# State tokens of a maxout kernel: half of the slots of all eight batches in one tile, instead of all slots of four batches

## The chip, the cores and the metric

The kernel runs on one core of one Trainium2 chip. Its time is the device time of one execution in microseconds (us); several executions are timed and their median is given. One further execution was taken with the hardware profiler; all rows below come from that one. Engines are named as the profile names them: PE multiplies matrices, PEld loads its weights, DVE and ACT do element work and copies, POOL does copies and issues the casting loads, SP only issues DMAs and waits.

## The reference, cut to what matters

`x` has 8 batches, 8 heads, 512 tokens and 64 features a head; `state` has 32 slots in place of the 512 tokens. Each batch makes two attention reads, which stand one behind the other along the token axis, so that a batch has 512 + 32 = 544 rows of 512 features. Each row then goes through a maxout layer.

```python
scores  = scale * np.matmul(x, state.transpose(0, 1, 3, 2))
a       = softmax(scores)
xread   = np.matmul(a, state)                   # 8 x 8 x 512 x 64
scores2 = scale * np.matmul(state, x.transpose(0, 1, 3, 2))
a2      = softmax(scores2)
sread   = np.matmul(a2, x)                      # 8 x 8 x 32 x 64
attn_out = np.concatenate([xread, sread], axis=2)
x = attn_out.transpose(0, 2, 1, 3).reshape(8 * 544, 512)
h = np.maximum(np.maximum(x @ w1, x @ w2), x @ w3)   # 768 wide
return h @ w_out                                     # 4352 x 512, float32
```

The last 32 of each batch's 544 rows are the state tokens: 8 x 32 = 256 rows in all, 512 KB of the output.

## The kernel before

The work is a list of operations written out by hand (FIRST, EACH for batches 2 to 6, LAST), performed in that order; each engine's queue keeps the order, and the waits between engines follow from the tiles. Batches go through scores, exponentials, weights, transposes, the first layer (three matmul groups a piece of 128 features, `pw`, and a maximum over them by ACT and DVE into `ht`), the second layer (`po`) and a store of the rows (`osb`).

The state read of a batch (`sread`, `sread_scale`) gives 128 partitions (4 pairs of heads by 32 slots) by 128 features. A DMA transpose on SP (`sread_turn`, L343) turns it into `ats[:, b]`, with the features of a pair of heads on the partitions and 4 x 32 columns. `sread_place` (L348) then copies these 128 columns into `atp`, the state tokens of all batches: POOL does it for seven batches and ACT for batch 5. Of `atp` each of the 4 pairs of heads has 256 columns, one for a state token. In the kernel before, a column's place is (half j of the batches, slot n, batch within the half).

When all eight batches have been placed, the first layer for the state tokens runs in LAST (`l1s 0` to `l1s 5`, `layer1_states`): 6 pieces of 12 matmuls that stream all 256 columns of a pair of heads. The result `hts` is 128 x 6 x 256. The second layer takes 128 of the 256 columns at a time as weights (`l2p s j c0 c1`: tile j, features c0 to c1), so that row p of the result is column 128j + p of `atp`. The result is copied to `osb["s"][:, j, c0:c1]` by ACT or DVE (`layer2_part_out`, L463) and stored by `store_part` (L467): five DMAs, two on ACT's queue and three on SP's, of 128, 128, 256, 128 and 384 features. The last operation of LAST is the store of 384 features of tile 0 on SP, 128 rows of 1536 bytes.

`state_rows(j)` is the output side of these stores. Before, it is the 32 slots of four batches, slot outermost: 32 steps of 2048 bytes, in each 4 steps of a batch (544 x 2048 bytes). The other side is 128 partitions of `osb`.

Behind LAST stands a branch on `flag` to a fallback that is not taken in these runs (L593). It holds uses of the same functions with DVE copies (`sread_turn_mm`) and whole-row stores of the state tokens. After it, at L658, SP waits in turn for the completion of each DMA semaphore, and the engines meet at barriers; there the program ends.

Of the kernel before, what the change touches and what calls it, by code (L numbers as in the profile page):

```python
# [10 lines left out]
BF16 = mybir.dt.bfloat16  # L11
# [63 lines left out]
def kernel(  # L75
# [10 lines left out]
    nc = tc.nc  # L86

    B, H, S, D = x.shape
    _, _, Ns, _ = state.shape
    HD = H * D  # L90
    SP = S + Ns
# [5 lines left out]
    J = 4  # L97
    HS = H // 2
# [5 lines left out]
    data = ctx.enter_context(tc.tile_pool(name="data", bufs=1))  # L104
# [5 lines left out]
    copier = {"D": nc.vector.tensor_copy, "A": nc.scalar.copy, "P": nc.gpsimd.tensor_copy}  # L110
    times = {"D": nc.vector.tensor_mul, "P": nc.gpsimd.tensor_mul}
# [14 lines left out]
    ones = const.tile([128, 128], BF16, name="ones")  # L126
    warm = const.tile([128, 1], F32, name="warm")
    ats = data.tile([128, B, HS, Ns], BF16, name="ats")
    atp = data.tile([128, HS, 2, Ns, 4], BF16, name="atp")
    seen = data.tile([128, B, J * H + 2], F32, name="seen")  # L130
    flag = data.tile([128, 1], I32, name="flag")

    xT, e, a, aT, G, ht, osb, xp = {}, {}, {}, {}, {}, {}, {}, {}
    open_ps = {}

    def new(d, b, shape, name, bufs=2):
        d[b] = work.tile(shape, BF16, tag=name, bufs=bufs, name=name)
# [4 lines left out]
    def bank(shape, dtype, name):  # L142
        return pp.tile(shape, dtype, tag="b" + next(homes["b"]), bufs=1, name=name)
# [104 lines left out]
    def parity(v, g):  # L248
        return v if g is None else v[:, :, g:g + 1]
# [18 lines left out]
    rdens = {}  # L268
# [8 lines left out]
    def weights(b, g, c):  # L277
        if not g:
            new(a, b, [128, J, 2, HS, Ns], "a")
        n = 2 if g is None else 1  # L280
        times[c](  # L281
            out=parity(a[b], g).rearrange("p j g s n -> p j (g s) n"),
            in0=parity(e[b], g).rearrange("p j g s n -> p j (g s) n"),
            in1=rdens.pop((b, g)).rearrange("p j g s -> p j (g s)").unsqueeze(3).to_broadcast(
                (128, J, n * HS, Ns)))

    def a_turn(b, g):
        if g == 0:
# [56 lines left out]


    def sread_place(b, c):
        copier[c](out=atp[:, :, b // 4, :, b % 4], in_=ats[:, b])  # L348

    def sread_turn_mm(b):  # L350
        p = bank([128, HS, Ns], BF16, "prt")
        nc.tensor.transpose(p.rearrange("p s n -> p (s n)"), srs.pop(b).rearrange("p g d -> p (g d)"), ident)
        nc.vector.tensor_copy(out=atp[:, :, b // 4, :, b % 4], in_=p)

# [108 lines left out]
    def store_part(b, j, c0, c1, q):  # L465
        if b == "s":
            queue[q].dma_start(out=state_rows(j)[:, :, c0:c1], in_=osb[b][:, j, c0:c1])  # L467
            return
        queue[q].dma_start(
            out=out[b * SP:b * SP + S, :].rearrange("(p j) f -> p j f", j=J)[:, j, c0:c1],  # L470
            in_=osb[b][:, j, c0:c1])
# [4 lines left out]
            in_=osb[b][:, j0:j1, :])  # L476

    def state_rows(j):
        return out.rearrange("(b t) f -> b t f", t=SP)[4 * j:4 * j + 4, S:SP, :].rearrange("b n f -> n b f")

    def store_states(j, q):
        queue[q].dma_start(out=state_rows(j), in_=osb["s"][:, j, :])
# [16 lines left out]
    def set_flag():  # L499
# [13 lines left out]
        "warm": (warm_exp, 0), "busy": (keep_busy, 0), "stc": (states_cast, 0), "stt": (states_turn, 0),  # L513
        "stp": (states_place, 0), "xt": (x_turn, 1), "xtc": (x_turned, 1), "xtd": (x_turn_dma, 1),
        "sc": (scores, 1), "ex": (exps, 1), "sum": (sums, 1), "wt": (weights, 1), "at": (a_turn, 1),
        "atc": (a_turned, 1), "atd": (a_turn_dma, 1), "pad": (pad, 1), "sr": (sread, 1),
        "srs": (sread_scale, 1), "srt": (sread_turn, 1), "ap": (sread_place, 1), "g": (g_slice, 1), "gc": (g_sliced, 1),
        "gr": (g_run, 1), "grc": (g_ran, 1), "l1": (layer1, 1), "l1s": (layer1_states, 0),
        "m0": (max_first, 1), "ma": (max_second, 1), "mb": (max_third, 1), "l2": (layer2, 1), "l2c": (layer2_out, 1),
# [73 lines left out]
    with tc.If(bad != 0, label="again"):  # L593
        for b in range(B):
            for d in (xT, e, a, aT, G, ht, osb, xp):
                d.pop(b, None)
            for g, c in ((0, "A"), (1, "D")):
                x_turn(b, g)
                x_turned(b, g, c)
            scores_below_max(b)  # L600
            sums(b)
            weights(b, None, "D")
            for g, c in ((0, "A"), (1, "D")):
                a_turn(b, g)
                a_turned(b, g, c)
            if b >= 2:
                pad(b)
            sread_below_max(b)
            sread_scale(b)
            sread_turn_mm(b)  # L610
            for m in range(NM):
                g_slice(b, m)
                g_sliced(b, m, "A")
            for m in range(NM):
                layer1(b, m)
                max_first(b, m)
                max_second(b, m)
                max_third(b, m)
            for j in range(J):
                layer2(b, j)  # L620
                layer2_out(b, j, "A")
                store(b, j, j + 1, "P")
# [40 lines left out]
```

## Time and profile before

| what | value |
|---|---|
| median of 3 timed executions | 156.05 us (155.54 to 156.09) |
| the profiled execution, its own time | 155.43 us |
| its span, first to last instruction | 153.5 us |
| PE busy | 145.8 us (95% of the span) |
| DVE busy | 110.0 us (72%) |
| ACT busy | 85.4 us (56%) |
| POOL busy | 52.3 us (34%) |
| granted TensorE clock, mean | 0.991 |
| L348, placing the state read of a batch | POOL x7, 469 ns; ACT x1, 493 ns |
| L467, stores of state tokens | 5 DMAs, 544 to 666 ns to issue |

The time of an execution holds some 1.9 us that lie outside the span. An engine's busy time is the sum of its instructions; a wait is put down to whatever ended it. A DMA is issued by an engine's queue (SPq, ACTq, POOLq) and lands later, when all its parts have been written; the time to landing counts from the issue.

### The profile page before, as it was taken

To read this page: it belongs to the slowest core of one execution; us is meant where nothing else is said; L and a number is where in the kernel's file an instruction comes from. 1 tells how busy PE (TensorE), PEld (TensorE's weight loads), DVE (VectorE), ACT (ScalarE), POOL (GpSimd) and SP (SyncE) were. 2 spreads that over 40 slices of the span, in tenths; PEclk is the share of its full clock that TensorE was granted. 3 is DMA by queue.
4 is the path that set the end of the run, shared out by engine and by line. 5 is a ranking of instruction groups with operands and counts; after the bars stand their busy time and mean duration, and the time that the engine had idled before them with its cause. 6 is when DMAs were issued, how large, how long until landed. Compare 5 with 4: busy or idle time off the path is not lost.

```text
span 153.5 us, 3632 instructions
## 1 busy us (share of the span) xinstructions
PE 145.8 (95%) x1434; PEld 73.2 (48%) x1434; DVE 110.0 (72%) x192; ACT 85.4 (56%) x140; POOL 52.3 (34%) x72
## 2 busy tenths in 40 slices
PE   6998899999999999999999999999999999999970
PEld 2565344343444444444444444444444445679850
DVE  1678968899898887688768876887688666852530
ACT  3536687764747474747474747475747344434220
POOL 6979829103996100916037003700320100000000
PEclk9999999999999999999999999999999999999996
DMA  4999999899999999932956094507030700107351
GB/s 104 241 197 200 199 194 182 125 214 189 157 136 263 199 193 284 243 82 63 295 123 73 2 297 120 75 7 274 4 68 14 279 6 4 68 2 269 111 192 60
DMA packets 39269, 22.30 MB, mean 145 GB/s; under 512 B 22096, under 2 KB 37200, under 8 KB 39248
## 3 DMA queue, kind: packets, MB, share of 16 engines
q0 software_dynamic: 13584, 7.60, 35.9%
q1 hardware_dynamic: 23792, 10.56, 30.9%
q10 hardware_dynamic: 1872, 3.87, 6.6%
q8 instruction: 12, 0.20, 0.5%
q14 instruction: 9, 0.07, 0.2%
HBM read 15.20 MB, written 8.91 MB: 157 GB/s over the span
## 4 chain that ended last, share of the span: by engine, by line
PE 75%; DMA 16%; DVE 2%; POOL 2%; issue 1%; ACT 1%; POOLq 0%
PE pw L413 37%; PE po L444 24%; DMA x<-in_x_dram 9%; DMA wout<-in_moe_w_out_dram 7%; PE po L459 5%; PE pg L360 4%; PE ps L259 2%; PE psr L324 1%; POOL xp L308 1%; DVE seen L273 1%; PE pgh L360 1%; DVE xT L241 1%; POOL a L281 1%; PE idle L208 1%; PE pxt L234 0%
## 5 line engine op out<-in xcount | busy, mean ns | idle before, releaser
L413 PE MATMUL pw<-aT,G 128*128 128x512 bf16 x288 | 66.4, 379 | 0.0
L433 DVE TENSOR_TENSOR t<-t,pw 128x512 bf16<-128x512 bf16 (+1 forms) x54 | 35.3, 654 | 15.4 <-ACT t L428 12.8
L428 ACT CAST t<-pw 128x512 bf16<-128x512 f32 (+1 forms) x54 | 30.4, 562 | 27.6 <-PE pw L413 26.9
L413 PEld LDWEIGHTS <-G 128*128 128x128 bf16 x288 | 27.2, 98 | 33.2 <-issue 1.7
L444 PE MATMUL po<-wout,ht 128*128 128x512 bf16 x168 | 40.2, 380 | 0.1
L437 DVE TENSOR_TENSOR ht<-t,pw 128x512 bf16<-128x512 bf16 x48 | 32.8, 686 | 4.7
L281 POOL TENSOR_TENSOR a<-e,rden 128x1024 bf16<-128x1024 bf16 (+1 forms) x10 | 15.7, 1568 | 42.1 <-ACT G L400 30.0
L444 PEld LDWEIGHTS <-ht 128*128 128x128 bf16 x168 | 15.2, 98 | 20.0 <-issue 2.1
L400 ACT CAST G<-pg 128x1024 bf16<-128x1024 f32 x22 | 21.8, 1018 | 4.7 <-PE pg L360 4.7
L273 DVE TENSOR_REDUCE seen<-e 128x32 f32<-128x1024 bf16 (+1 forms) x10 | 10.0, 1003 | 5.3 <-ACT e L266 5.3
L308 POOL COPY xp<-x 128x1024 bf16<-128x1024 bf16 x12 | 12.5, 1076 | 3.6 <-DMA x<-in_x_dram 3.6
L451 DVE COPY osb<-po 128x512 f32<-128x512 f32 x17 | 11.4, 669 | 2.9 <-PE po L444 2.8
L266 ACT ACTIVATE e<-ps 128x1024 bf16<-128x1024 f32 (+1 forms) x10 | 8.4, 852 | 7.8 <-PE ps L259 7.8
L360 PE MATMUL pg<-w,bd 64*32 64x512 bf16 (+1 forms) x288 | 11.2, 363 | 0.9 <-DMA w<-in_moe_w_dram 0.9
L348 POOL COPY atp<-ats 128x128 bf16<-128x128 bf16 x7 | 3.2, 470 | 23.9 <-DMA ats<-sr 23.9
L451 ACT COPY osb<-po 128x512 f32<-128x512 f32 x11 | 6.5, 587 | 7.9 <-PE po L444 7.9
L167 POOL DMA_DIRECT2D x<-in_x_dram x13 | 10.1, 791 | 0.9 <-POOLq L647 0.9
L378 ACT CAST G<-pg 128x768 bf16<-128x768 f32 x10 | 8.0, 803 | 2.0 <-PE pg L360 1.9
L208 PE MATMUL idle<-zero 128*128 128x512 bf16 x25 | 7.6, 444 | 1.4 <-DVE zero L186 1.3
L413 PE MATMUL pw<-atp,w 128*128 128x256 bf16 x72 | 8.7, 273 | 0.0
L413 PEld LDWEIGHTS <-w 128*128 128x128 bf16 x72 | 6.9, 98 | 1.2
L463 ACT COPY osb<-po 128x128 f32<-128x128 f32 (+2 forms) x11 | 3.4, 315 | 6.8 <-PE po L459 6.7
(61 smaller groups left out, 100.8 us busy)
## 6 DMA issues: line engine op xcount, KB each, us to landing
x<-in_x_dram POOLq DMA_DIRECT2D x13, 256.0 KB, 9.4
out_dram<-osb ACTq DMA_DIRECT2D x6, 512.0 KB, 4.0
out_dram<-osb SPq DMA_DIRECT2D x5, 512.0 KB, 2.9
w<-in_moe_w_dram POOLq DMA_DIRECT2D x5, 256.0 KB, 9.3
w<-in_moe_w_dram POOLq DMA_DIRECT2D x2, 384.0 KB, 9.5
wout<-in_moe_w_out_dram POOLq DMA_DIRECT2D x1, 768.0 KB, 10.4
out_dram<-osb SPq DMA_DIRECT2D x3, 256.0 KB, 2.1
osb<-in_x_dram SPq DMA_DIRECT2D x1, 512.0 KB, 3.8
```

The source lines that it names most:

```text
L167: nc.gpsimd.dma_start(out=x_part(b, g), in_=x_heads(b, g))
L273: nc.vector.reduce_sum(out=den, in_=parity(e[b], g), axis=AX.X)
L281: times[c](out=parity(a[b], g).rearrange("p j g s n -> p j (g s) n"), in0=parity(e[b], g).rearrange("p j g s n -> p j (g s) n"), in1=rdens ...
L308: nc.gpsimd.tensor_copy(out=xp[b][:, :, :, g * (D + 1):g * (D + 1) + D], in_=v[:, g])
L360: nc.tensor.matmul(p(s, g), bd(b, 2 * s + g)[64 * g:64 * g + 64, g, :], f(w_sb[64 * g:64 * g + 64, s]), start=True, stop=True, tile_positi ...
L400: copier[c[g]](out=v[:, g:h], in_=p[:, g:h, 0:c1 - c0])
L413: nc.tensor.matmul(pw[i][:, 0:n], lhs(i, k), rhs(k), start=(k == 0), stop=(k == nk - 1))
L428: nc.scalar.copy(out=t0s[b, m][:, 0:n], in_=open_ps["l", b, m][0][:, 0:n])
L433: nc.vector.tensor_max(t1s[b, m][:, 0:n], t0s.pop((b, m))[:, 0:n], open_ps["l", b, m][1][:, 0:n])
L437: nc.vector.tensor_max(ht[b][:, m, :], t1s.pop((b, m))[:, 0:n], open_ps.pop(("l", b, m))[2][:, 0:n])
L444: nc.tensor.matmul(p, ht[b][:, m, j * 128:(j + 1) * 128], wout_sb[:, m, :], start=(m == 0), stop=(m == NM - 1))
L451: copier[c[i]](out=o[:, j, i * w:i * w + w], in_=p[:, i * w:i * w + w])
```

## The change

`atp` has its 256 columns in another order: (half j of the slots, batch, slot within the half), so a tile of 128 state tokens is 16 slots of all eight batches, batch outermost. The copies at L348 (and the DVE copies of the fallback) write runs of 16 neighbouring columns instead of single columns at a distance of 4. The output side of the state stores becomes 8 batches (steps of 544 x 2048 bytes) outermost and in each 16 neighbouring rows (steps of 2048 bytes). The number of matmuls, copies and stores, their order on every queue and their waits are the same. `weights` gets a form that can deal its work to several engines; every call in the lists names one engine, for which the loop runs once and issues what was issued before.

```diff
-    atp = data.tile([128, HS, 2, Ns, 4], BF16, name="atp")
+    atp = data.tile([128, HS, 2, B, Ns // 2], BF16, name="atp")
...
     def weights(b, g, c):
         if not g:
             new(a, b, [128, J, 2, HS, Ns], "a")
-        n = 2 if g is None else 1
-        times[c](
-            out=parity(a[b], g).rearrange("p j g s n -> p j (g s) n"),
-            in0=parity(e[b], g).rearrange("p j g s n -> p j (g s) n"),
-            in1=rdens.pop((b, g)).rearrange("p j g s -> p j (g s)").unsqueeze(3).to_broadcast(
-                (128, J, n * HS, Ns)))
+        n, r = 2 if g is None else 1, rdens.pop((b, g))
+        for i in range(len(c)):
+            j = slice(i * J // len(c), (i + 1) * J // len(c))
+            times[c[i]](
+                out=parity(a[b], g)[:, j].rearrange("p j g s n -> p j (g s) n"),
+                in0=parity(e[b], g)[:, j].rearrange("p j g s n -> p j (g s) n"),
+                in1=r[:, j].rearrange("p j g s -> p j (g s)").unsqueeze(3).to_broadcast(
+                    (128, J // len(c), n * HS, Ns)))
...
     def sread_place(b, c):
-        copier[c](out=atp[:, :, b // 4, :, b % 4], in_=ats[:, b])
+        copier[c](out=atp[:, :, :, b], in_=ats[:, b].rearrange("p s (j n) -> p s j n", j=2))
 
     def sread_turn_mm(b):
...
-        nc.vector.tensor_copy(out=atp[:, :, b // 4, :, b % 4], in_=p)
+        nc.vector.tensor_copy(out=atp[:, :, :, b], in_=p.rearrange("p s (j n) -> p s j n", j=2))
...
     def state_rows(j):
-        return out.rearrange("(b t) f -> b t f", t=SP)[4 * j:4 * j + 4, S:SP, :].rearrange("b n f -> n b f")
+        return out.rearrange("(b t) f -> b t f", t=SP)[:, S + Ns // 2 * j:S + Ns // 2 * (j + 1), :]
```

## The prediction

> **What bounds the kernel now.** I read the page's busy times and its chain first, then the groups that touch `atp` and the state stores (L348, L467), then SP's waits and the last five microseconds in order of time.
>
> ```profile
> span 153.5 us, 3632 instructions
> PE 145.8 (95%) x1434; PEld 73.2 (48%) x1434; DVE 110.0 (72%) x192; ACT 85.4 (56%) x140; POOL 52.3 (34%) x72
> ...
> PE 75%; DMA 16%; DVE 2%; POOL 2%; issue 1%; ACT 1%; POOLq 0%
> ```
>
> PE is the bound from its first matmul to its last. The change gives PE not one instruction more or less, so it can act in two places only: where PE waits for `atp`, and behind PE's last matmul. First the copies into `atp` and their readers (duration in ns: shortest, median, longest; then first and last start):
>
> ```profile
> L348 POOL COPY atp<-ats x7: 469/469/471, 61.5 to 122.7; 128x128 bf16<-128x128 bf16 x7
> L348 ACT COPY atp<-ats x1: 493/493/493, 126.5 to 126.5; 128x128 bf16<-128x128 bf16 x1
> ...
> L413 PE MATMUL pw<-atp,w x72: 272/273/273, 128.8 to 143.4; 128*128 128x256 bf16 x72
> ```
>
> POOL's last copy ends at 123.2 us, ACT's at 126.95, and PE first reads `atp` at 128.75: 5.6 and 1.8 us to spare. Next the end. These are the last instructions in order of time (start, duration), and SP's wait for the last store:
>
> ```profile
> 147.79 0.81 PE L459 MATMUL po<-wout,hts 128*128 128x384 bf16 x4
> 147.96 0.26 PEld L459 LDWEIGHTS <-hts 128*128 128x128 bf16 x2
> 148.12 0.39 SPq L469 DMA_DIRECT2D out_dram<-osb  x1
> 148.65 0.48 ACT L463 COPY osb<-po 128x384 f32<-128x384 f32 x1 [2.21 <-PE po L459]
> 149.15 0.54 SPq L467 DMA_DIRECT2D out_dram<-osb  x1
> ```
>
> ```profile
> SPq L658 <- DMA out_dram<-osb: 0.5, 1, 0.5
> ```
>
> ```profile
> L467 SPq DMA_DIRECT2D out_dram<-osb x3: 544/658/666, 146.5 to 149.1; - x3
> ...
> L467 ACTq DMA_DIRECT2D out_dram<-osb x2: 547/592/637, 146.3 to 147.6; - x2
> ...
> DMA to landing us min/median/max: 2.1/2.2/3.4
> ```
>
> PE ends at 148.6, ACT copies the last 128x384 piece, SP issues its store at 149.15, and 4.4 us more pass to the end. In them two things run side by side. SP loads the flag, takes the branch and checks one DMA semaphore after another; it reaches that of the last store at 152.04. The store itself lands 3.4 us after its issue, at 152.53, though the median state store lands after 2.2. So the end hangs on this store, but only by the 0.5 us in SP's wait; behind it lie another 0.98 us of barriers.
>
> The packets in the trace tell why it is late. It is 128 packets of 1536 bytes. On each of the 16 DMA engines eight run one behind the other, 61 ns apart, as in the 128x384 store before it whose output has 128 rows in one step. Of the store's 16 completions twelve come from 151.21 to 151.35 us; then stragglers at 151.71, 151.91, 152.06 and 152.53. The last one's engine fetched a 16 KB block of instructions from 149.25 to 150.79 (a packet of the instruction queue of 1541 ns), then did the eight rows of the store ahead (landing 151.97), and only then these eight. The one at 152.06 was held up in the same way behind an 8 KB fetch.
>
> **The change, part by part.**
>
> *Copies into `atp`.* Eight copies change form: the same 128 columns, now 8 runs of 16 in place of single columns 4 apart. No row shows the new form. Below: the 128x1024 POOL copy (L308) takes 1076 ns, so (1076 - 469) / 896 = 0.68 ns a column and 383 ns fixed; a copy falls to 383 at the least, -0.09 us. Above: the whole 1076 ns of that row, +0.61 us. I take 469, the row with the same number of columns. Either end is covered on POOL: behind its copies stand only later batches' copies and weights, and it idles 23.9 us ahead of three of the copies for their DMA. On ACT one copy is behind cover of 0.71 us, its idle time ahead of the next copy of `po` at 127.66, and of 1.8 us to PE. Cost: nothing. If ACT's took over 1.2 us, that copy would start late, and beyond 2.3 us PE would.
>
> *Matmuls and layers.* 72 matmuls at 272 ns read the same 256 neighbouring columns; which token a column is changes no shape. The `hts` maxima (410 to 422 ns), the second layer and the copies L463 are as they were. `weights` issues the same ten instructions. Waits on all queues are unchanged. Cost: nothing, with no cover needed.
>
> *Issue of the five state stores.* Now 544 to 666 ns on the queue. The nearest rows are those of L469, whose output has 128 steps in one dimension: 332 to 426 ns. The new output has two dimensions like the old one. Bounds: -0.21 us (544 - 332) and +0.12 (666 - 544) for each; I take 0, the row with two dimensions. ACT's stores have nothing urgent behind them. SP has 0.64 us idle between the issue of the store at 148.12 and that at 149.15, so only the last store's own issue is on the path.
>
> *Transfer of the last store.* Rows, bytes and packet size are as before; how they are dealt to the DMA engines may not be. The output's outermost count was 32, dealt to 16 engines at two each; it becomes 8. Bounds: still 16 engines at 8 rows, +0; or one engine for each outermost step, eight at 16 rows, 8 x 61 = +0.49 us on each engine used. No row of this trace has an outermost count under 16, so neither is shown. I take eight engines, because the old 32 is dealt out evenly and 8 can't be dealt to 16 without splitting a step. The skill speaks against this change here: the Trainium skill, DMA: Bandwidth & Descriptors, section "Why a DMA increments its semaphore by 16 and not by 1", has the number of engines as the largest up to 16 that divides the slowest dimensions of both sides. By that rule 32 and 128 gave 16 engines, with which the trace's 16 chains of eight packets agree, and 8 and 128 give eight; the sum by the rule has the +0.49, without it +0.
>
> What 0.49 us costs depends on which engines these are. An undisturbed engine lands at 151.35 + 0.49 = 151.84, before SP looks at 152.04: hidden. If the engine that ended last (152.53) is used, it lands at 153.02: +0.49 at the end. If it is not used but the one of 152.06 is, that lands at 152.55: +0.02. If neither is, SP finds everything landed at 152.04: -0.49, and that is a floor, since the store ahead, still on all 16 engines, lands at 151.97. Engines start a store in a fixed order, seven within 27 ns and nine 53 to 145 ns after the first; in a store on ACT at 142.89 the engine behind on account of the previous fetch is missing among the nine. The one held up by the 8 KB fetch is missing among the seven. If the eight that are used are about the seven that start first, the late one drops out and the 8 KB one stays: +0.02. I take this, for want of a better sign.
>
> *The four earlier state stores.* They last landed at 149.72 and the queue is empty between them: 16 rows of 512 bytes at 24 ns are 0.19 us more, 16 of 1024 bytes 0.34 more, all before SP asks.
>
> Sum: 0 + 0 + 0 + 0.02 on the profiled execution's 155.43 us (span 153.5 and 1.93 outside). The median of the runs, 156.05, is 0.62 above that execution; the same difference on the median gives 156.1.
>
> **The rivals.** A difference of 0.5%, 0.78 us, is about what a measurement of this kernel can tell from no change.
>
> A. *The late engine is among the eight.* For: half of 16 engines are used, and the code fetch will come again at the same place. Against: the order of starts above. +0.49: 156.54, still within 0.5%.
>
> B. *Slower for good: a row takes longer.* An engine's 16 rows now come from 16 neighbouring partitions and go to one 32 KB stretch of the output, instead of to four batches; if that halves its speed, 122 ns a row, the store takes 16 x 122 = 1.95 us for 0.49. An undisturbed engine would land at 152.81, +0.28; the late one, if used, at 153.99, +1.46: 157.5. For: in the disturbed stretch of the tail single packets do take 107 to 399 ns. Against: rows of 1536 bytes take 61 ns both in the store to four batches and in the 128-row store. It passes 0.5% with the late engine used and 16r - 0.49 > 0.78, at r = 79 ns a row.
>
> C. *Faster: both held-up engines drop out.* -0.49, and -0.21 more if the issue falls to 332 ns, because SP's own chain then starts that much earlier: -0.70, 155.35. Against: the two stand in different groups of starts, so eight of 16 rarely miss both.
>
> D. *The store still goes to 16 engines.* +0: 156.05. For: every store in the trace does.
>
> **How the numbers follow.** Chances: the forecast 0.40, A 0.24, B 0.15, C 0.12, D 0.09. In C half lies beyond 0.5% with the spread of the runs (155.54 to 156.09): faster 0.06. B, and the tenth of A that this spread carries over (0.03), make slower 0.18. The rest is 0.76. The range goes from C without the cheaper issue, 155.55, to A with half of the runs' spread (0.27) on top, 156.8; left out are most of B and the end of C, about 2 in 10.
>
> **What would show it.** Copies at L348 between 383 and 1076 ns with PE's first read of `atp` no later after the matmul before it. State stores whose packets run in eight chains of 16, not 16 of eight, 61 ns apart for 1536 bytes. Issue of L467 near 0.55 to 0.66 us. SP's wait for the last store: about 0.5 us as forecast, 1.0 in A, none in C. The forecast is wrong if PE's last matmul moves, or if SP's checks before the last one move: the branch's own code fetch would then compete with longer stores.

## The result, and the profile after

The changed kernel takes 156.97 us (median of 22 executions) beside 156.04 us for the kernel before (22 executions, taken in turns). The ratio is 1.0052, 95% interval 1.003 to 1.0075: slower, by about half of one per cent. The ratio and its interval leave out three of the 22 executions of the changed kernel, which fell into a slower state that both kernels show now and then; without them its median is 156.58 us. A second series gave 1.0045 (1.0008 to 1.0082). The prediction was 156.1 us, with 155.55 to 156.8 as its range.

From the page of the changed kernel: its span, its busy times and the DMA queues of SP (q1) and ACT (q10), with packets, MB and share of 16 engines' time:

```profile
span 154.4 us, 3632 instructions
PE 146.0 (95%) x1434; PEld 73.3 (48%) x1434; DVE 109.9 (71%) x192; ACT 85.1 (55%) x140; POOL 51.5 (33%) x72
...
q1 hardware_dynamic: 23768, 10.56, 30.4%
q10 hardware_dynamic: 1856, 3.87, 6.6%
```

The same two lines of the kernel before:

```profile
q1 hardware_dynamic: 23792, 10.56, 30.9%
q10 hardware_dynamic: 1872, 3.87, 6.6%
```

All engines work as long as they did; the span is 0.9 us longer. The bytes are equal, but q1 has 24 packets less and q10 has 16 less. SP issues three state stores and ACT two, and in the traces every DMA engine that takes part in a store ends its share with one small packet of 4 bytes. Each store has lost eight of these (3 x 8 on q1, 2 x 8 on q10): it runs on 8 engines and not on 16.

The copies into `atp` and their reader in the changed kernel:

```profile
L350 POOL COPY atp<-ats x7: 287/291/293, 61.4 to 122.7; 128x128 bf16<-128x128 bf16 x7
L350 ACT COPY atp<-ats x1: 311/311/311, 126.5 to 126.5; 128x128 bf16<-128x128 bf16 x1
...
L415 PE MATMUL pw<-atp,w x72: 272/273/273, 128.8 to 143.4; 128*128 128x256 bf16 x72
```

The copies are 0.18 us shorter and PE reads no sooner: 128.8 us in both kernels. Next the end in order of time, then SP's waits at L660 (L658 before; sum, times, longest), then the issue of the state stores (ns: shortest, median, longest):

```profile
148.17 0.34 SPq L471 DMA_DIRECT2D out_dram<-osb  x1
148.69 0.48 ACT L465 COPY osb<-po 128x384 f32<-128x384 f32 x1 [2.21 <-PE po L461]
149.19 0.61 SPq L469 DMA_DIRECT2D out_dram<-osb  x1
```

```profile
SPq L660 <- DMA out_dram<-osb: 1.1, 2, 0.9
```

```profile
L469 SPq DMA_DIRECT2D out_dram<-osb x3: 609/612/762, 146.5 to 149.2; - x3
...
L469 ACTq DMA_DIRECT2D out_dram<-osb x2: 614/900/1187, 146.3 to 147.6; - x2
```

Up to the issue of the last store the kernels are alike to 0.05 us (149.15 and 149.19). Everything that was lost lies behind it: SP waits 0.9 us for the last store where it was 0.5, and it comes to that wait later. From the trace's packets and completions of the last store:

| us from the last store's issue | before | changed | changed, second profile |
|---|---|---|---|
| engines | 16 | 8 | 8 |
| first row starts | 1.21 | 1.25 | 1.25 |
| rows over 80 ns, longest | 4, 349 ns | 28, 568 ns | 27, 521 ns |
| first completion | 2.06 | 3.11 | 3.07 |
| store ahead (16 engines) completes | 2.82 | 3.30 | 2.86 |
| last completion | 3.38 | 4.23 | 4.07 |
| SP's flag load takes | 0.998 | 1.252 | 1.295 |

A row is one packet of 1536 bytes, and a completion is an engine's report that its share has landed. The earliest of the engines is already 1.0 us later than before, and the last one 0.7 to 0.85.

### The profile page after: what moved, and what is told of

The parts are those of the page before. It is cut to its first block, busy times and chain, and to the rows that moved or that the text cites. A ratio compares the mean times of both kernels' runs of the same rounds, so it can differ in the third digit from the quotient of the medians.

```text
span 154.4 us, 3632 instructions
## 1 busy us (share of the span) xinstructions
PE 146.0 (95%) x1434; PEld 73.3 (48%) x1434; DVE 109.9 (71%) x192; ACT 85.1 (55%) x140; POOL 51.5 (33%) x72
## 4 chain that ended last, share of the span: by engine, by line
PE 79%; DMA 12%; DVE 2%; POOL 2%; ACT 1%; issue 0%; DVEq 0%
PE pw L415 37%; PE po L446 24%; DMA wout<-in_moe_w_out_dram 7%; DMA x<-in_x_dram 6%; PE po L461 5%; PE pg L362 4%; PE idle L208 4%; PE ps L259 2%; PE psr L326 1%; POOL xp L310 1%; DVE seen L273 1%; PE pgh L362 1%; DVE xT L241 1%; POOL a L283 1%; PE pxt L234 1%; PE pt L219 1%
## 5 line engine op out<-in xcount | busy, mean ns | idle before, releaser
L350 POOL COPY atp<-ats 128x128 bf16<-128x128 bf16 x7 | 2.0, 290 | 24.1 <-DMA ats<-sr 24.0
```

## The experiments

The runs are to tell these theories apart. **N**: the number of engines, and with it the rows on each, sets the end. **P**: rows are slow because of where eight batches' rows go. **F**: slow rows come from what the branch sets off. Four more came up on the way, all on why an engine's first rows are slow: **A** and **O** (the distance between the engines' addresses in the output), **E** (eight engines as such) and **R** (the partitions that are read). Theory A is not the prediction's rival A.

### The changed kernel again

No edit.

> The changed kernel once more, for a second look at its tail. Theory N (number of engines: the five state stores run on 8 DMA engines with 16 rows each, and the end follows the latest of these): 8 completions for each state store, SP's wait for the last store near 0.9 us as in the first profile, time +0.8 us (+0.5%) over before. Theory P (place: rows are slow because eight batches' rows, 544 x 2048 bytes apart, are written at the same time): the same time, but rows of the state stores at over 61 ns (1536 bytes) throughout the store, also where no instruction fetch or flag load is under way.

1.0045 (1.0008 to 1.0082), 156.67 us. SP's wait:

```profile
SPq L660 <- DMA out_dram<-osb: 0.9, 1, 0.9
```

As N expects, in the time, in the wait and in the 8 engines of each state store. The slow rows come at the start only; from the fifth row of an engine on they take 61 ns, so the form of P with slow rows throughout falls.

### Half of the slots, slot outermost

```diff
-    atp = data.tile([128, HS, 2, B, Ns // 2], BF16, name="atp")
+    atp = data.tile([128, HS, 2, Ns // 2, B], BF16, name="atp")
...
-        copier[c](out=atp[:, :, :, b], in_=ats[:, b].rearrange("p s (j n) -> p s j n", j=2))
+        copier[c](out=atp[:, :, :, :, b], in_=ats[:, b].rearrange("p s (j n) -> p s j n", j=2))
...
-        return out.rearrange("(b t) f -> b t f", t=SP)[:, S + Ns // 2 * j:S + Ns // 2 * (j + 1), :]
+        return out.rearrange("(b t) f -> b t f", t=SP)[:, S + Ns // 2 * j:S + Ns // 2 * (j + 1), :].rearrange("b n f -> n b f")
```

> Tiles of half of the slots of all eight batches as in the change, but slot outermost and batch within, so the output side is 16 steps of 8. Theory N: 16 completions for each state store, 8 rows on an engine, the last store lands about 3.3 us after its issue or earlier, time as before within 0.3% (ratio 0.997 to 1.003). Theory P: eight batches are still written side by side, the time stays at the change's +0.5%. The copies into atp go back to about 470 ns (columns 8 apart) in both.

0.9963 (0.9929 to 0.9997): the price is gone. Tiles hold the same tokens as in the change; only the order within a tile went back to slot outermost. The copies, the landing of the state stores and SP's wait:

```profile
L350 POOL COPY atp<-ats x7: 755/757/919, 61.9 to 123.1; 128x128 bf16<-128x128 bf16 x7
L350 ACT COPY atp<-ats x1: 777/777/777, 127.0 to 127.0; 128x128 bf16<-128x128 bf16 x1
```

```profile
DMA to landing us min/median/max: 2.1/2.3/3.6
```

```profile
SPq L660 <- DMA out_dram<-osb: 0.5, 1, 0.5
```

There are 16 completions a store and SP's wait is 0.5 us again. P falls as well: the eight batches are still written side by side, and the price is gone. The copies are not "about 470 ns" as expected but 757 (columns 8 apart, where the kernel before had them 4 apart), and it costs nothing that the time shows. The first rows of the last store took up to 199 ns here, on 16 engines: a slow start isn't a matter of eight engines alone.

### All slots of four batches, batch outermost

```diff
-    atp = data.tile([128, HS, 2, Ns, 4], BF16, name="atp")
+    atp = data.tile([128, HS, 2, 4, Ns], BF16, name="atp")
...
-        copier[c](out=atp[:, :, b // 4, :, b % 4], in_=ats[:, b])
+        copier[c](out=atp[:, :, b // 4, b % 4], in_=ats[:, b])
...
-        return out.rearrange("(b t) f -> b t f", t=SP)[4 * j:4 * j + 4, S:SP, :].rearrange("b n f -> n b f")
+        return out.rearrange("(b t) f -> b t f", t=SP)[4 * j:4 * j + 4, S:SP, :]
```

> Tiles of all slots of four batches as before the change, but batch outermost, so the output side is 4 steps of 32. Theory N: 4 completions for each state store, 32 rows on an engine, 32 x 61 = 1.96 us a store where it was 0.49: an undisturbed engine ends the last store at about 152.8 us of the span, a late one at 154.0 or more; time +1.0 to +2.3 us over before (ratio 1.006 to 1.015), more than the change. Theory P: four batches as before, time as before (ratio 0.998 to 1.002).

1.0194 (1.0128 to 1.026), 159.1 us: 3.1 us over before, more than N's upper end. Its profiled execution took 167.68 us, where the others took 158.66 to 160.62, and in it PE waits 5.1 us for a DMA near 50 us; so only its tail is read:

```profile
SPq L658 <- DMA out_dram<-osb: 3.5, 3, 2.5
```

```profile
q1 hardware_dynamic: 23756, 10.56, 27.8%
q10 hardware_dynamic: 1848, 3.87, 6.4%
```

These are another 12 and 8 packets less than in the change: four engines a store. The last store lands 6.7 us after its issue; its 32 rows on an engine start three microseconds after the issue, behind the stores ahead of it, and the first take up to 342 ns. The direction and the order (16, 8, 4 engines: 0, +0.5, +1.9%) are N's; the size shows that rows on an engine at 61 ns are not the whole price, since N's upper end of 2.3 us was reckoned with them.

### Both kernels without flag load, branch and fallback

```diff
-    bad = nc.values_load(flag[0:1, 0:1], min_val=0, max_val=1,
-                         skip_runtime_bounds_check_because="flag is the result of a comparison")
-    homes["b"], homes["w"] = cycle("0123"), cycle("01")
-    with tc.If(bad != 0, label="again"):
...
-                store_states(j, "P")
```

> The changed kernel without the flag's loads, the branch and the fallback behind it (the fallback is left out, the rest is whole). No engine loads the flag and none jumps. Theory N: the 16 rows of each engine in the last store run at 61 ns from the first to the last, it lands about 2.7 us after its issue (2.2 of the median state store before plus 0.49), and the end hangs on it. Theory F (fetches: the rows that took 107 to 568 ns in the change's last store were slowed by what the branch sets off): no row over 80 ns here. Theory P: rows over 80 ns here too.

> The kernel before without the flag's loads, the branch and the fallback (left out, the rest is whole). Theory N with F: 16 engines, 8 rows at 61 ns, no stragglers beyond 0.2 us; the run is shorter than the changed kernel without the fallback by 0.4 to 0.6 us, that is by the eight rows more (0.49) and not by the 0.9 us that the two kernels' profiles differ by. Theory P: shorter by 0.8 us or more.

Changed: 155.62 us, 0.9949 (0.9894 to 1.0003) of the kernel before; before: 154.41 us, 0.9857 (0.9812 to 0.9903). SP's waits at the end, of the changed kernel, then of the kernel before, both without the fallback:

```profile
SPq L571 <- DMA out_dram<-osb: 2.1, 2, 1.8
```

```profile
SPq L569 <- DMA out_dram<-osb: 0.8, 1, 0.8
```

Here the change costs 1.2 us (four executions of each), more than in the whole kernel and more than the 0.4 to 0.6 of N. Without the branch the kernel before has no straggler: 16 completions from 2.04 to 2.30 us after the issue, no row over 65 ns. The changed kernel's last store completes from 3.05 to 3.65 us after the issue, and 29 of its rows take over 80 ns, up to 418. F falls: with no branch and no code fetch within the store's rows the slow rows are there. What P had named for these two runs, slow rows and 0.8 us or more, did come, but its reason had fallen with the slot outermost. The fallback hides a part of the price. With it the last store of the kernel before lands 3.38 us after its issue and not 2.30, because one of its 16 engines fetches code first; the changed store lands after 4.23 and 4.07 and not 3.65, a smaller loss, and its eight engines don't include the one of the longest fetch (see below).

### The state store not last

```diff
-    sop s 0 384 512 A; l2p 7 2 256 512;
-    l2pc 7 2 256 512 D; l2p s 0 0 384; sop s 1 128 256 S; sop s 1 256 512 S; sop 7 2 256 512 S;
-    l2pc s 0 0 384 A; sop s 0 0 384 S;
+    sop s 0 384 512 A; l2p s 0 0 384;
+    l2pc s 0 0 384 A; l2p 7 2 256 512; sop s 1 128 256 S; sop s 1 256 512 S; sop s 0 0 384 S;
+    l2pc 7 2 256 512 D; sop 7 2 256 512 S;
```

> The changed kernel with the last two pieces exchanged: the 384 features of state tile 0 are multiplied, copied and stored ahead of the 256 features of batch 7's tile 2, so a store of 128 rows in one dimension (16 engines, 332 ns to issue, 46 ns a row) comes last. Theory N: the state store's 16 rows run beside the last piece's matmuls, and the change's price falls by more than half: ratio to before 0.997 to 1.002. If instead the end hangs on SP's own chain of loads and checks, it ends as the change does.

> The kernel before with the same exchange. Theory N: 16 engines either way; the issue of the last store falls from 544 to 332 ns, its rows from 61 to 42 ns, and the piece ahead of it is 128x256 instead of 128x384 to copy (0.42 on DVE against 0.48 on ACT): up to 0.5 us less than before, ratio 0.996 to 1.0. If stragglers alone set the end, as before within 0.2%.

> The kernel before with the last two pieces exchanged, again, to narrow its interval: the store of state rows no longer comes last. The first look gave 0.9964 (0.9929 to 1.0). If the gain is that of the shorter last store, 0.996 to 0.999; if it was the spread of the stragglers, 0.999 to 1.001.

On the changed kernel: 1.0002 (0.996 to 1.0044) of the kernel before, within N's expectation; the interval is too wide to say how much of the price is gone. On the kernel before: 0.9964 (0.9929 to 1.0) and, again, 1.0018 (1.0 to 1.0036): no gain that holds. The shorter issue that was expected there (332 ns) did not come: in both profiles of the exchanged kernel before, the last store takes 1.65 and 1.70 us to issue, and why wasn't looked into. So the exchange may hide a slow store, but it makes no faster kernel than the one before.

### The slow first rows: distance in the output

The changed kernel without the fallback, its state stores in a tensor of their own (so the state rows of the output are not written), the pitch of the batches varied. The lines shown are those for 548 rows:

```diff
-        return out.rearrange("(b t) f -> b t f", t=SP)[:, S + Ns // 2 * j:S + Ns // 2 * (j + 1), :]
+        return apart.rearrange("(b t) f -> b t f", t=SP + 4)[:, S + Ns // 2 * j:S + Ns // 2 * (j + 1), :]
...
+    apart = nc.dram_tensor("apart", (B * (SP + 4), d_model), F32, kind="Internal").ap()
```

> The changed kernel without flag loads, branch and fallback, and its five state stores go to a tensor of their own whose batches stand 544 rows of 2048 bytes apart, as in the output (the state rows of the output are not written; the fallback is left out). Theory A (addresses: engines that write at the same time to rows a multiple of 64 KB apart hold each other up until they have drifted apart): the first rows of each state store take up to 400 ns as in the run without the fallback and it ends about 3.6 us after the issue. Theory E (engines: any store on 8 engines starts slowly, whatever it writes): the same.

> As the run before it, but the batches of the tensor apart stand 548 rows apart, so that the eight engines write 8 KB from one another within 64 KB instead of a multiple of 64 KB apart (the state rows of the output are not written; the fallback is left out). The engines, partitions, rows and bytes are the same. Theory A: all rows of 1536 bytes take 61 to 65 ns, the store lands about 0.6 to 0.8 us sooner after its issue than with 544. Theory E: the slow first rows stay, no difference.

> As the two before, with batches 545 rows apart: the eight engines write 2 KB from one another, within 16 KB (the state rows of the output are not written; the fallback is left out). Theory A: between the two, rows of up to 200 ns at the start, as in the store with the slot outermost, whose 16 engines also wrote 2 KB apart. Theory E: the same slow first rows as with 544.

The last store completes 3.63, 3.53 and 3.51 us after its issue with pitches of 544, 548 and 545 rows; 29, 28 and 29 rows take over 80 ns, the longest 409, 342 and 342. Theory A expected 0.6 to 0.8 us less with 548: it falls.

> Changed kernel without the fallback, state stores to a tensor apart (the state rows of the output are not written; the fallback is left out): 8 steps, 64 KB from one another, of 16 neighbouring rows. The stores of a batch write from engines 64 KB apart too and take 61 ns a row from the first. Theory O (output side: engines that write a megabyte apart start slowly): rows at 61 to 65 ns, last store landing within 3.0 us of its issue. Theory E (eight engines or what they read): first rows of 100 to 400 ns as with 544, 545 and 548 rows, landing 3.5 us or more after the issue.

> The same with 16 steps, 544 rows from one another, of 8 rows: 16 engines, each in its own megabyte (the state rows of the output are not written; the fallback is left out). Theory O: slow first rows. Theory E: 61 to 65 ns a row, landing about 2.2 us after the issue as in the kernel before without the fallback.

> The same with 32 steps, 544 rows from one another, of 4 rows: 16 engines with two steps each, the shape of the store before but far apart (the state rows of the output are not written; the fallback is left out). Theory O: slow first rows. Theory E: as the kernel before without the fallback, 61 to 65 ns a row. Were this fast and the one with 16 steps of 8 slow, the number of steps an engine gets would decide and not the distance.

> Changed kernel without the fallback, stores to the tensor apart with 544 rows between batches, the last store in two DMAs of 64 partitions, each 8 steps of 8 rows (the state rows of the output are not written; the fallback is left out). The engines stay eight and write as far apart as in the change, but read partitions 8 apart at a time and not 16 apart. Theory R (reading side, partitions 16 apart): the first of the two runs at 61 to 65 ns a row. Theory O and theory E in its number of engines: its first rows are slow as before.

Each of these four was executed once, so only the rows of its trace are read and not its time. The output side is `t=32` with 16 rows (f1), `t=544` with 8 rows in 16 steps (f2), with 4 rows in 32 steps (f3), and for f4 the pitch of 544 with the last store in two:

```diff
+            if c1 - c0 == 384:
+                for k in range(2):
+                    queue[q].dma_start(out=state_rows(j)[:, 8 * k:8 * k + 8, c0:c1],
+                                       in_=osb[b][64 * k:64 * k + 64, j, c0:c1])
+                return
```

The landing times of the state stores in f2, then in f3:

```profile
DMA to landing us min/median/max: 2.0/2.2/2.6
```

```profile
DMA to landing us min/median/max: 2.0/2.1/2.2
```

The last state stores, each row of 1536 bytes, sorted by the rows in one outer step (for f4 the first of its two halves, 64 rows; the kernel with 16 x 8 rows and the one with 4 x 32 still have the fallback):

| outer steps x rows | engines | kernel | rows over 80 ns | longest row | last completion after issue |
|---|---|---|---|---|---|
| 32 x 4 | 16 | before, no fallback | 0 of 128 | 65 ns | 2.30 us |
| 32 x 4, far apart | 16 | f3 | 0 | 65 | 2.22 |
| 16 x 8 | 16 | slot outermost | 52 | 199 | 3.62 (a late engine) |
| 16 x 8, far apart | 16 | f2 | 57 | 159 | 2.59 |
| 8 x 8 | 8 | f4 | 31 of 64 | 145 | 2.48 |
| 8 x 16 | 8 | changed, no fallback | 29 | 418 | 3.65 |
| 8 x 16, 64 KB apart | 8 | f1 | 29 | 389 | 3.56 |
| 4 x 32 | 4 | four batches, batch outermost | 10 | 342 | 6.70 |

Theory O falls: f3 writes as far apart as f2 and is fast, f1 writes 64 KB apart as the batch stores do and is slow. E in its number of engines falls too: f2 has 16 and starts slowly, as f4 with eight does, and f4's longest row is a third of that in the 8 x 16 stores. R's "61 to 65 ns" for f4 was wrong as well. What goes with the slow start is the number of rows that an engine takes in one step: none slow with 4, up to 199 ns with 8, up to 568 with 16. The store with 32 (up to 342) doesn't fit into this order, but its rows start 3 us after the issue, behind other stores. Eight rows on an engine are not enough by themselves: the 128x384 store of batch 7, 128 steps of one row on 16 engines, has no row over 66 ns in any of the runs. Whether it is the reading of neighbouring partitions or the making of the list of packets that takes the time isn't told apart by these runs; it stays open.

## Why the prediction was wrong, point by point

*What bounds the kernel.* Right: nothing moved up to the last store's issue, and all 0.9 us are behind it.

*Copies into `atp`.* Right that they cost nothing, wrong in the lower bound: 291 and 311 ns, below the 383 that was worked out from a row of another form. The old form, columns 4 apart, is the slow one, so a fixed part can't be worked out from it and a copy of another form.

*Matmuls, layers, `weights`.* As predicted.

*Issue.* The last store's went from 544 to 609 ns, inside the bounds. ACT's first state store went from 637 to 1187 ns, far outside (+0.12), with nothing urgent behind it. SP's flag load behind the last issue went from 0.998 to 1.252 us, which the prediction had not reckoned with. SP comes to its last check 3.37 us after the issue and not 2.89: 0.07 of this is the issue, 0.25 the load and 0.16 a wait for the store ahead, which landed later. So the floor "152.04" moved by half a microsecond, and SP's earlier checks moved with it, which the prediction had named as a sign of being wrong. Why the load is longer was not tried.

*Transfer: eight engines.* Right. The completions show it: 32 and 16 outer steps gave 16 engines, 8 gave 8 and 4 gave 4. The Trainium skill's rule in DMA: Bandwidth & Descriptors, section "Why a DMA increments its semaphore by 16 and not by 1", held in every form tried.

*Size of a row: the step that failed.* The prediction put sixteen rows at 61 ns each, from stores of another form, and so had +0.49 us on each engine used. In the changed store only the rows from an engine's fifth on take 61 ns; nearly all of the first four take over 80, up to 568. An undisturbed engine needs 1.5 to 1.65 us for its sixteen rows, 93 to 103 ns each, and the first completion comes 1.0 us later than before (3.11 and 3.07 us against 2.06). Without the fallback this is the same, 3.05 against 2.04, so neither the branch nor the fetch makes it. For the engine that ends last the forecast was 152.55 us, 3.40 after the issue. Measured are 4.23 and 4.07, which is 0.67 to 0.83 later. In the first profile this engine gets to its twelve rows of 61 ns only at 152.24, behind rows of 340 and 134 ns. Of the 1.2 us without the fallback, 0.49 are the eight rows more, and the slow start is the likely rest.

*Which engines.* The forecast had the engine of the 16 KB fetch drop out, and in both profiles of the change it did, so this part held, on a sign that the prediction itself called weak. Before, this engine ends its rows of the store ahead 2.33 us after the last issue and has its eight rows of the last store behind them, one every 61 ns up to 2.83. In the changed kernel the fetch runs from 150.32 to 151.31 us, and its eight rows of 1024 bytes follow up to 152.00. No row of the last store starts there next: six of the eight engines are done by 152.11, the seventh takes a row every 61 ns from 151.94 on, and the eighth has a row under way from 151.79, so both had begun before 152.00. In the second profile the fetching engine is done with the store ahead 2.39 us after the issue, and the two engines that end last have only 12 and 14 of their sixteen rows starting after that. So rival A, whose 156.54 us lies near the measured time, isn't what happened, and a time near it would have been luck.

*Rival B* (0.15) has the right kind of cause and the wrong form: it asked whether every row takes longer, at 122 ns, and found 79 ns the point where it decides. Its price was worked out for an undisturbed engine and for that of the 16 KB fetch only; on the engine that the forecast itself kept it would have been 152.06 + 1.46 = 153.52 us, and 153.42 was measured. The stretch of output that B named as a reason isn't it: with the slot outermost an engine's eight rows go to eight batches, in f2 to one stretch, and both start slowly.

*The four earlier state stores.* They were reckoned at 0.19 to 0.34 us more; the last of them landed at 150.58 and not at 149.72. That is before SP's first check at 151.69, so SP doesn't wait for it.

*D and C* are out: the stores do not go to 16 engines, and of the two late engines that C wanted gone the last store still has stragglers, 0.7 to 0.8 us behind the sixth of its eight completions.

## What to carry to other kernels

Before changing the order of rows in a tile, look at the outermost count of the DMA on its other side: the order of two dimensions decided between 16, 8 and 4 engines and between 0, +0.5 and +1.9%, while which tokens share a tile did not matter. A last store is priced by its latest engine and not by its bytes, so count the rows on one engine and ask what holds that engine up. A row's time that was read in a store of one form needn't hold in another; and a rival that changes this time has to be worked out on the engine that the forecast keeps, too. What already holds up the end (here a code fetch) hides a part of such a price, and shows it when it goes: 0.8 us with the fallback, 1.2 us without.

## What the runs showed of the hardware that was not expected

- A POOL copy of 128x128 bf16 takes 291 ns when it writes runs of 16 or 32 columns, 469 with columns 4 apart and 757 with columns 8 apart; ACT takes 311, 493 and 777.
- A store on eight or four engines has one more completion than engines in the trace: about 1.0 us after the last store's issue, ahead of its first row at 1.25, one update comes that belongs to no row.
- A store starts slowly according to the rows that an engine takes in one outer step: 65 ns a row with 4, up to 199 with 8, up to 568 with 16, and 61 again from about the fifth row of an engine on. With 32 it was seen only behind other stores (up to 342).
- A fetch of 16 KB of instructions (1.0 to 1.5 us) holds up the rows of an ordinary store that stand behind it: in all five profiles with the branch and a state store last, the last completion of the store ahead comes 1.1 to 2.0 us after the bulk of its 16. Without the branch all 16 come within 0.1 us in the kernel before. That the rows share an engine with the fetch is read from their times, since the trace doesn't number the engines.
